# An attention stage set anew in a fused attention and two-layer kernel: q scaled in its cast, row sums inverted in one go, new keys

## The chip, the cores and the metric

The kernel runs on one core of one Trainium2 chip. The metric is the time of one execution on the device in microseconds (us); the kernel before has a median of 741.01 us in three runs (741.01 to 741.36). Five engines work side by side: TensorE (PE, matrix products; PEld is its loading of weights), VectorE (DVE), ScalarE (ACT), GpSimd (POOL) and SyncE (SP), which here issues nearly all DMAs. Each runs its own list of instructions in order and waits on semaphores for the others. SBUF is the working memory with 128 partitions, PSUM the memory that PE writes into, in banks.

## The reference

```
scores = (q @ k.T) / sqrt(64), for 2 x 8 heads of 768 tokens, 64 wide
scores = -1e9 where the six sign bits of q @ proj and of k @ proj differ
attn   = softmax(scores);  x = attn @ v, heads side by side: 1536 x 512
h = x @ w_in (512 x 2048);  x = (h * tanh(softplus(h))) @ w_out
h = x @ w_in2;              out = (h - tanh(h)) @ w_out2
```

## The kernel before, in words

**Products in parts.** Every operand of a product is split into a high part (a cast to a shorter float) and a low part (the operand less its high part), and a product is high x high + high x low + low x high.

**Attention.** Heads are handled in eight pairs g, each with heads h = 0, 1. Transposed q and k of a pair lie as 128 x 768 tiles; `halves_split` (line 413) makes qh, ql, kh, kl from them in halves of 384 columns. For the first pair ScalarE and VectorE do it. For the others GpSimd makes kh, kl and ql, while ScalarE first scales q in place (line 423) and then casts it to qh (line 430). `piece` (line 467) makes three matmuls per half for the sign bits, which go to a tile z. `stack` (line 499) gathers by eight DMAs per head the rows of qh, ql, kh, kl and z into four tiles a, b, c, d, so that a score tile (128 queries x 768 keys) is four matmuls: b,a and d,c for 512 keys, then for 256 (lines 582, 583). They go into the tile s, of which PSUM holds one. A few tiles of the start (`SPLIT_S`) go into two small banks pt instead.

`scores` (line 566): VectorE clamps a tile out of PSUM into a buffer p and takes its row minimum (line 586); ScalarE takes the exponential and the row sums (line 609). `chunk` (line 631): PE transposes three tiles p for one chunk of 128 keys (line 643); then either ScalarE writes the high part ph (line 659) and VectorE the low part pl (line 662), or, in the chunks of `POOL_C`, ScalarE copies to f (line 651) and GpSimd makes ph and pl (line 655). PE multiplies them with the values vt (lines 622, 623), four chunks later. `gather` (line 669) adds the two parts of the result to u; `inverse` (line 681) inverts the row sums of one half of the queries (three small VectorE ops, lines 691 to 695) and spreads them through DRAM by six DMAs (lines 701, 705) into a tile r; `finish` (line 710) multiplies u by r and splits the outcome into xh and xl, on GpSimd save for the last pair.

**Two expert layers.** In blocks of 16 units, with products of seven instead of eight blocks; their weights come as 64-bit integers and are converted (`to_float`, lines 820 to 850), some of it during attention.

**The order.** No engine's list is written by hand. Every step is an `op` with an engine, a cost, a key and what it reads and writes. `Plan.order` (line 196) walks a clock: at each moment it picks, for the engine that can start first, the step with the smallest key among those that can start within `EPS` of the first. Keys of the attention count in ticks (`TICK`, 24 per pair, `at`); `AHEAD` says how many ticks a score tile comes ahead of its transposes, `STACK`, `VALUES`, `LOAD` when in a pair the DMAs and values are due. `LATE`, `LATS`, `LATG` are the latencies that the planner adds between engines; `RATE` and `ISSUE` price DMAs. The numbers at the top of the file thus decide the place of each instruction.

## Time and profile before

| | us |
|---|---|
| median of three runs | 741.01 |
| profiled execution | 740.89 |
| its span, first to last instruction | 739.1 |
| PE busy | 727.7 (98%) |
| PEld busy | 673.6 (91%) |
| VectorE busy | 643.8 (87%) |
| ScalarE busy | 529.7 (72%) |
| GpSimd busy | 179.7 (24%) |

Shares are of the span. Attention fills about the first 230 us, the expert layers the rest; GpSimd works in the first part only. A matmul's row is as long as the matmul is in the engine, and the next one starts before it ends, so its cost is read from start to start. The granted clock of PE is at its higher level in every slice of the page. In a row of the timeline "[0.31 <-POOL kh L375]" says that the engine idled 0.31 us before it, until that instruction of GpSimd.

### The profile page before, as it was taken

To read this page: it belongs to the slowest core of one execution; us is meant where nothing else is said; L and a number is where in the kernel's file an instruction comes from. 1 tells how busy PE (TensorE), PEld (TensorE's weight loads), DVE (VectorE), ACT (ScalarE), POOL (GpSimd) and SP (SyncE) were. 2 spreads that over 40 slices of the span, in tenths; PEclk is the share of its full clock that TensorE was granted. 3 is DMA by queue.
4 is the path that set the end of the run, shared out by engine and by line. 5 is a ranking of instruction groups with operands and counts; after the bars stand their busy time and mean duration, and the time that the engine had idled before them with its cause. 6 is when DMAs were issued, how large, how long until landed. Compare 5 with 4: busy or idle time off the path is not lost.

```text
span 739.1 us, 13094 instructions
## 1 busy us (share of the span) xinstructions
PE 727.7 (98%) x4382; PEld 673.6 (91%) x4382; DVE 643.8 (87%) x1372; ACT 529.7 (72%) x1140; POOL 179.7 (24%) x224
## 2 busy tenths in 40 slices
PE   7999999999999999999999999999999999999998
PEld 4889999999999999999999999998998899999997
DVE  6988998998999999999898899789898775767893
ACT  6989999999997866767676676666565445466660
POOL 5677987988961000000000000000000000000000
PEclk9999999999999999999999999999999999999999
DMA  7775775785562655545655567999986786735621
GB/s 215 184 200 130 204 201 129 204 211 126 156 175 88 231 197 168 172 156 179 204 181 186 185 232 247 330 330 329 350 295 251 270 278 232 244 144 186 222 87 64
DMA packets 59390, 150.96 MB, mean 204 GB/s; under 512 B 7990, under 2 KB 20406, under 8 KB 59324
## 3 DMA queue, kind: packets, MB, share of 16 engines
q1 hardware_dynamic: 58892, 149.65, 63.9%
q8 instruction: 34, 0.56, 0.3%
q10 hardware_dynamic: 432, 0.49, 0.2%
q14 instruction: 32, 0.26, 0.1%
HBM read 88.18 MB, written 43.04 MB: 178 GB/s over the span
## 4 chain that ended last, share of the span: by engine, by line
PE 93%; DVE 2%; DMA 2%; ACT 2%; issue 1%; POOL 0%; ACTq 0%; SPq 0%; DVEq 0%; POOLq 0%
PE pt L1023 11%; PE pt L1025 11%; PE pt L1024 11%; PE pt L643 8%; PE pt L1101 6%; PE pt L1113 6%; PE s L1100 6%; PE pt L1100 6%; PE pt L1338 5%; PE s L582 4%; PE pt L622 4%; PE pt L623 4%; PE s L583 4%; PE s L1338 3%; PE s L1113 3%; DVE p L586 1%
## 5 line engine op out<-in xcount | busy, mean ns | idle before, releaser
L1023 PE MATMUL pt<-xh,a 128*128 128x384 f32 x288 | 96.7, 336 | 0.0
L1025 PE MATMUL pt<-xh,a 128*128 128x384 f32 x288 | 96.7, 336 | 0.0
L1024 PE MATMUL pt<-xl,a 128*128 128x384 f32 x288 | 96.6, 335 | 0.0
L586 DVE TENSOR_SCALAR_CACHE_REDUCE p<-s 128x768 f32<-128x768 f32 x93 | 88.2, 948 | 7.6 <-PE s L583 5.7
L609 ACT ACTIVATE p<-p,mn 128x768 f32<-128x768 f32 x96 | 90.7, 945 | 3.1 <-DVE p L586 2.0
L662 DVE TENSOR_TENSOR pl<-pt,ph 128x384 fp32r<-128x384 f32 x148 | 78.5, 546 | 8.6 <-ACT ph L659 7.6
L643 PE MATMUL pt<-cst,p 128*128 128x128 f32 x576 | 83.8, 272 | 1.1 <-DVE pl L662 1.1
L643 PEld LDWEIGHTS pt<-cst,p 128*128 128x128 f32 x576 | 69.5, 140 | 6.1 <-DVE pl L662 1.4
L659 ACT CAST ph<-pt 128x384 fp32r<-128x384 f32 x148 | 68.8, 484 | 5.2 <-PE pt L622 3.1
L1101 PE MATMUL pt<-gh,o 128*128 128x256 f32 x256 | 71.7, 280 | 0.0
L622 PE MATMUL pt<-ph,vt 128*128 128x384 f32 x192 | 70.4, 367 | 0.3 <-ACT f L651 0.2
L582 PE MATMUL s<-b,a 128*128 128x512 f32 (+1 forms) x186 | 68.2, 367 | 1.1 <-DVE p L586 0.7
L623 PE MATMUL pt<-pl,vt 128*128 128x384 f32 x192 | 64.9, 338 | 0.4 <-DVE pl L662 0.4
L583 PE MATMUL s<-d,c 77*128 77x512 f32 (+3 forms) x186 | 59.3, 340 | 0.6 <-ACT raw L846 0.6
L802 DVE TENSOR_TENSOR gl<-pl,gh 128x384 fp32r<-128x384 f32 x96 | 52.4, 551 | 6.5 <-ACT gh L1047 6.5
L1023 PEld LDWEIGHTS pt<-xh,a 128*128 128x128 f32 x288 | 54.1, 188 | 3.3 <-ACT pl L1042 0.2
L1024 PEld LDWEIGHTS pt<-xl,a 128*128 128x128 f32 x288 | 54.1, 188 | 1.3
L1025 PEld LDWEIGHTS pt<-xh,a 128*128 128x128 f32 x288 | 54.1, 188 | 0.1
L1047 ACT CAST gh<-pl 128x384 fp32r<-128x384 f32 x96 | 48.7, 514 | 2.1 <-DVE pl L802 1.1
L1101 PEld LDWEIGHTS pt<-gh,o 128*128 128x128 f32 x256 | 48.3, 189 | 0.0
L1061 ACT COPY ph<-pt 128x384 f32<-128x384 f32 x56 | 26.9, 481 | 28.7 <-PE pt L1025 28.6
L1100 PE MATMUL pt<-gh,o 128*128 128x512 f32 x128 | 47.2, 391 | 0.0
(301 smaller groups left out, 2080.7 us busy)
## 6 DMA issues: line engine op xcount, KB each, us to landing
w<-w SPq DMA_DIRECT2D x52, 512.0 KB
raw<-in_moe_w_in_dram SPq DMA_DIRECT2D x32, 512.0 KB
raw<-in_moe_w_out_dram SPq DMA_DIRECT2D x32, 512.0 KB
split<-a SPq DMA_DIRECT2D x24, 512.0 KB
a<-split SPq DMA_DIRECT2D x24, 512.0 KB
w<-t SPq DMA_DIRECT2D x32, 256.0 KB
o<-split SPq DMA_DIRECT2D x24, 256.0 KB
b<-kh SPq DMA_DIRECT2D x30, 192.0 KB
```

The source lines that it names most:

```text
L582: nc.tensor.matmul(o, a()[:, tok], b_()[:, kc], start=True, stop=False)
L583: nc.tensor.matmul(o, c_()[used, tok], d_()[used, kc], start=False, stop=True)
L586: nc.vector.tensor_scalar(out=out, in0=in_, scalar1=MASKED, scalar2=None, op0=ALU.min, op1=ALU.min, accum_out=low)
L609: lambda: nc.scalar.activation(out=p(), in_=p(), func=AF.Exp, bias=mn(), scale=-1.0, accum_out=sm()[:, h, t:t + 1],),
L622: nc.tensor.matmul(o()[:, :HB], vt()[:, c, :], ph()[:, :HB], start=(c == 0), stop=False)
L623: nc.tensor.matmul(o()[:, :HB], vt()[:, c, :], pl()[:, :HB], start=False, stop=(c == NT - 1))
L643: nc.tensor.transpose(pt()[:, t * P:(t + 1) * P], ps[t]()[:, c * P:(c + 1) * P], ident)
L1023: nc.tensor.matmul(o, tl()[:, 0, c], at_(0, kk), start=start and kk == 0, stop=False, skip_group_check=not start)
L1024: nc.tensor.matmul(o, tl()[:, 0, c], at_(1, kk), start=False, stop=False, skip_group_check=not start)
L1025: nc.tensor.matmul(o, tl()[:, 1, c], at_(0, kk), start=False, stop=kk == 1, skip_group_check=not start)
L1100: nc.tensor.matmul(a()[:, n, :], w()[:, y, c], flat[x][:, :SEG], start=st, stop=sp)
L1101: nc.tensor.matmul(r()[:, 0, rest], w()[:, y, c], flat[x][:, SEG:], start=st and d % 2 == 0, stop=sp, skip_group_check=True)
```

## The change

The high part of q is written by ScalarE with the scale in the same instruction, for every pair and not only the first, and its low part is made by VectorE from the unscaled q. The row sums of both halves of a pair are inverted together (12 columns instead of 6, four stores and two spreads for a pair), but for the last pair; both halves of a pair are then finished after its second half. One more chunk per head goes by way of GpSimd, save in the last pair. The identity for the transposes is copied to a tile of its own, and the two columns of constants that stay in use are loaded once more. There are eight p buffers instead of six, and one wide r instead of two. The numbers of the planner for the attention are set anew. `MOVED` is empty, so the code that it guards emits nothing.

```
-POOL_C = ((1, 4), (4,))
+POOL_C = ((1, 4), (1, 4))
-SPLIT_S = (1, 3, 5)
+SPLIT_S = (1, 2, 4)
-T_BUFS, P_BUFS, U_BUFS = 4, 6, 3
+T_BUFS, P_BUFS, U_BUFS = 4, 8, 3
+MOVED = ((), ())
-Q_SCALE = "ACT"
-EPS = 0.0
+EPS = 0.145
-AHEAD = 9
+AHEAD = 11
...
-STACK = 12
-VALUES = 11
-LOAD = 15
...
+STACK = 17
+VALUES = 16
+LOAD = 14
...
-            if nm == "q" and g:
-                if Q_SCALE == "ACT":
-                    op("ACT", 0.42, k0 - 0.1, lambda c=c: nc.scalar.activation(out=raw()[:, c], in_=raw()[:, c], func=AF.Copy, scale=-SCALE), [], [(raw, i)])
...
-                op("ACT", 0.42, k0, lambda c=c: nc.scalar.copy(th()[:, c], raw()[:, c]), [(raw, i)], [(th, i)])
-            elif nm == "q":
+            if nm == "q":
                 op(
                     "ACT", 0.38, k0, release=Q_REL if (g, i) == (0, 1) else 0.0, fn=
                     lambda c=c: nc.scalar.activation(out=th()[:, c], in_=raw()[:, c], func=AF.Copy, scale=-SCALE),
...
-            if nm == "q" and not g:
+            if nm == "q":
                 op(
-                    "DVE", 0.47 if g == 0 else 0.6, k0 + 0.1,
+                    "DVE", 0.47, k0 + 0.1,
                     lambda c=c: nc.vector.scalar_tensor_tensor(
                         out=tl()[:, c], in0=raw()[:, c], scalar=-SCALE, in1=th()[:, c],
                         op0=ALU.mult, op1=ALU.subtract,
...
-        ("u", "u", U_BUFS), ("r", "r", 2), ("rt", "rt", 2), ("small", "mn mn2 sums", 6),
+        ("u", "u", U_BUFS), ("r", "r", 1), ("rt", "rt", 2), ("small", "mn mn2 sums", 6),
...
+            op("POOL", 0.25, 6.0, lambda: pool_copy(ident, land[:, 0, 0:P]))
...
-    def inverse(g, half, key):
+    def inverse(g, halves, key):
...
+        i0, nh = halves[0], len(halves)
+        rd, n = rds[i0], nh * 2 * TB
...
+            lambda: nc.vector.tensor_tensor(out=used(), in0=sm()[:, :, i0:i0 + nh], in1=tiny[:, :, :nh], op=ALU.add),
...
-                nc.sync.dma_start(out=r()[h * D:(h + 1) * D], in_=d[h:h + 1].to_broadcast([D, HB]))
+                nc.sync.dma_start(out=r()[h * D:(h + 1) * D, i0 * HB:(i0 + nh) * HB], in_=d[h:h + 1].to_broadcast([D, nh * HB]))
...
-                if h == 1:
-                    inverse(g, half, at(NT * n - 2))
+                if h == 1 and (half or g == len(pairs) - 1):
+                    inverse(g, (half,) if g == len(pairs) - 1 else (0, 1), at(NT * n - 2))
...
-                    if h == 1:
+                    if h == 1 and g == len(pairs) - 1:
                         finish(g, half, u, key + 0.3)
+                    elif h == 1 and half:
+                        for i in range(2):
+                            finish(g, i, us[i], key + 0.3 + i)
...
-    nc.scalar.dma_start(out=cst, in_=cst_d)
+    nc.scalar.dma_start(out=land[:, 0, 0:P + 66], in_=cst_d)
+    nc.scalar.dma_start(out=cst[:, 0:2], in_=cst_d[:, P:P + 2])
```

On PE, in the start: from the score tiles of the first queries to the first transposes (pt<-cst,p before; pt<-ident,p in the changed file, whose lines are numbered a little lower here). Before:

```order
L478 MATMUL pt<-qh,pjh 64x384
L479 MATMUL pt<-qh,pjl 64x384
L480 MATMUL pt<-ql,pjh 64x384
L478 MATMUL pt<-kh,pjh 64x384
L479 MATMUL pt<-kh,pjl 64x384
L480 MATMUL pt<-kl,pjh 64x384
L643 MATMUL pt<-cst,p 128x128 x6
```

And after:

```order
L471 MATMUL pt<-qh,pjh 64x384
L472 MATMUL pt<-qh,pjl 64x384
L473 MATMUL pt<-ql,pjh 64x384
L471 MATMUL pt<-kh,pjh 64x384
L472 MATMUL pt<-kh,pjl 64x384
L473 MATMUL pt<-kl,pjh 64x384
L471 MATMUL pt<-kh,pjh 64x384
L472 MATMUL pt<-kh,pjl 64x384
L473 MATMUL pt<-kl,pjh 64x384
L644 MATMUL pt<-ident,p 128x128 x3
```

A second piece of k, of the next pair, now stands ahead of the first transposes, and only three of these follow before the next score tile.

On PE, in the fourth pair, between two score tiles (s<-b,a for 512 keys is the first matmul of a tile). Before:

```order
L582 MATMUL s<-b,a 128x512
L583 MATMUL s<-d,c 128x512
L582 MATMUL s<-b,a 128x256
L583 MATMUL s<-d,c 128x256
L622 MATMUL pt<-ph,vt 128x384
L623 MATMUL pt<-pl,vt 128x384
L622 MATMUL pt<-ph,vt 128x384
L623 MATMUL pt<-pl,vt 128x384
L643 MATMUL pt<-cst,p 128x128 x3
L582 MATMUL s<-b,a 128x512
```

And after, between two tiles of the fifth pair:

```order
L575 MATMUL s<-b,a 128x512
L576 MATMUL s<-d,c 128x512
L575 MATMUL s<-b,a 128x256
L576 MATMUL s<-d,c 128x256
L619 MATMUL pt<-ph,vt 128x384
L620 MATMUL pt<-pl,vt 128x384
L644 MATMUL pt<-ident,p 128x128 x3
L619 MATMUL pt<-ph,vt 128x384
L620 MATMUL pt<-pl,vt 128x384
L644 MATMUL pt<-ident,p 128x128 x3
L575 MATMUL s<-b,a 128x512
```

Two products of the values and two runs of transposes lie between the tiles here, where two products and one run lay; each pair of the new order, from the third to the seventh, has the same distances between its tiles.

On GpSimd before, in the fourth pair, where the low part of q is made:

```order
L454 TENSOR_TENSOR kl<-k,kh 128x384 x2
L719 TENSOR_TENSOR u<-u,r 128x384
L454 TENSOR_TENSOR ql<-q,qh 128x384
L375 TENSOR_SCALAR xh_134<-u 128x384
L375 TENSOR_SCALAR ph<-f 128x384
L726 TENSOR_TENSOR xl_138<-u,xh_134 128x384
```

And on VectorE after, where it is made now:

```order
L579 TENSOR_SCALAR p,mn<-s 128x768
L437 SCALAR_TENSOR_TENSOR ql<-q,qh 128x384
L663 TENSOR_TENSOR pl<-pt,ph 128x384
L579 TENSOR_SCALAR p,mn<-s 128x768
L676 TENSOR_TENSOR u<-pt,f 64x384
L663 TENSOR_TENSOR pl<-pt,ph 128x384
```

The subtraction stands between two clamps of score tiles now.

## Rows read from the trace of the kernel before

**Rows 1.** Windows: us, PE, PEld, DVE, ACT, POOL busy (count), PEclk, DMA share, GB/s.

```profile
0.00:25.00 25.00, 18.78 (x85) 13.47 (x85) 18.64 (x47) 18.03 (x35) 15.52 (x25) 1.00 0.82 222
25.00:60.00 35.00, 34.42 (x221) 30.40 (x221) 29.92 (x68) 32.65 (x74) 27.19 (x35) 1.00 0.74 185
60.00:225.00 165.00, 164.85 (x1088) 151.74 (x1087) 153.24 (x342) 159.32 (x354) 135.11 (x164) 1.00 0.64 166
225.00:245.00 20.00, 19.55 (x125) 18.52 (x124) 19.57 (x45) 15.06 (x34) 1.85 (x2) 1.00 0.44 151
245.00:739.00 494.00, 490.09 (x2872) 459.44 (x2870) 422.45 (x875) 304.62 (x648) 0.00 (x0) 1.00 0.64 220
```

**Rows 2.** Timeline of PE, 113 to 117 us: start, duration, instruction [idle before].

```profile
113.90 0.49 PE L643 MATMUL pt<-cst,p 128*128 128x128 f32 x3
114.14 0.48 PE L582 MATMUL s<-b,a 128*128 128x512 f32 x1
...
114.93 0.34 PE L622 MATMUL pt<-ph,vt 128*128 128x384 f32 x1
115.11 0.34 PE L623 MATMUL pt<-pl,vt 128*128 128x384 f32 x1
...
115.64 0.49 PE L643 MATMUL pt<-cst,p 128*128 128x128 f32 x3
116.15 0.50 PE L582 MATMUL s<-b,a 128*128 128x512 f32 x1
```

**Rows 3.** Timeline of DVE, the clamp of the tile at 114.14.

```profile
115.13 0.96 DVE L586 TENSOR_SCALAR_CACHE_REDUCE p<-s 128x768 f32<-128x768 f32 x1 [0.49 <-PE s L583]
```

**Rows 4.** Groups by form, 45 to 210 us: count, busy us, mean ns, idle before.

```profile
L423 ACT ACTIVATE q<-q 128x384 f32<-128x384 f32 x10 | 5.5, 550 | 0.0
...
L662 DVE TENSOR_TENSOR pl<-pt,ph 128x384 fp32r<-128x384 f32 x108 | 57.4, 546 | 6.7 <-ACT ph L659 6.0
...
L691 DVE TENSOR_TENSOR rd<-sums,tiny 128x6 f32<-128x6 f32 x12 | 2.7, 228 | 0.0
L695 DVE STREAM_TRANSPOSE rt<-rd 128x32 f32<-128x32 f32 x12 | 2.5, 204 | 0.0
L694 DVE RECIPROCAL rd<-rd 128x6 f32<-128x6 f32 x12 | 2.2, 181 | 0.1
...
L655 POOL TENSOR_TENSOR pl<-f,ph 128x384 fp32r<-128x384 f32 x36 | 37.5, 1041 | 1.8
L375 POOL TENSOR_SCALAR ph<-f 128x384 fp32r<-128x384 f32 x36 | 18.9, 524 | 17.2 <-ACT f L651 14.2 <-PE pt L623 2.0 <-PE pt L643 0.5
...
L454 POOL TENSOR_TENSOR ql<-q,qh 128x384 fp32r<-128x384 f32 x12 | 12.0, 1017 | 0.0
```

**Rows 5.** Line 444 alone: count, ns minimum/median/maximum, first and last start.

```profile
L444 DVE SCALAR_TENSOR_TENSOR ql<-q,qh x2: 553/556/559, 5.3 to 13.0; 128x384 fp32r<-128x384 f32 x2
```

**Rows 6.** Window of one pair, first score tile to first score tile.

```profile
120.65:147.97 27.32, 27.32 (x183) 25.09 (x182) 25.11 (x57) 26.51 (x61) 22.96 (x29) 1.00 0.75 191
```

**Rows 7.** Timeline of PE in the start.

```profile
16.30 0.39 PE L480 MATMUL pt<-kl,pjh 128*64 128x384 f32 x1 [1.47 <-POOL kl L454]
...
21.24 0.55 PE L643 MATMUL pt<-cst,p 128*128 128x128 f32 x3 [1.14 <-DVE pl L662]
```

**Rows 8.** Timeline of POOL in the start: both halves of kl.

```profile
15.25 2.07 POOL L454 TENSOR_TENSOR kl<-k,kh 128x384 fp32r<-128x384 f32 x2 [0.56 <-DMA d<-kl]
```

**Rows 9.** Timeline of SP: start and length of an issue.

```profile
9.26 0.62 SPq L381 DMA_DIRECT2D d<-kl  x1
...
111.94 0.84 SPq L381 DMA_DIRECT2D c<-z  x1
```

**Rows 10.** Timeline of PE: the first score tile of the fifth pair.

```profile
120.65 0.48 PE L582 MATMUL s<-b,a 128*128 128x512 f32 x1
```

**Rows 11.** Lines 600 and 838 alone, columns as in rows 5.

```profile
L600 DVE TENSOR_TENSOR mn<-mn,mn x3: 145/151/1037, 13.4 to 22.5; 128x1 f32<-128x1 f32 x3
...
L838 DVE SCALAR_TENSOR_TENSOR w<-raw,w x6: 668/680/1074, 54.8 to 193.4; 128x512 uint32<-128x512 uint32 x6
```

More of the change, by code (lines that the diff above doesn't have):

```diff
@@ L63 @@
 SPARE = 1
-LATE = 0.22
-LATS = 0.15
-LATG = 0.5
+LATE = 0.28
+LATS = 0.2
+LATG = 0.6
 LATF = 0.3
-TICK = 1.11
-T_ATT = 8.0
-M0 = 7.0
-AHEAD = 9
+TICK = 1.1
+T_ATT = 7.0
+M0 = 2.0
+AHEAD = 11
 PV_LAG = 4
 PIECE = 2.5
-STACK = 12
-VALUES = 11
-LOAD = 15
-FIRST = (0.0, 1.0, 2.0, 6.0)
-V_REL = 15.0
-Q_REL = 9.5
-Z_REL = 12.5
+STACK = 17
+VALUES = 16
+LOAD = 14
+FIRST = (1.0, 0.0, 2.0, 6.0)
+V_REL = 12.0
+Q_REL = 8.0
+Z_REL = 9.5
 FILL = 3
@@ L369, in tile_lsh_attention_moe @@
     hot = plan.pools["f"].tile([P, XB], F32R, tag="f", name="hot")
+    land = plan.pools["w32"].tile([P, 2, DM], F32, tag="w3", name="land")
+    pj = land[:, 0, P + 2:P + 66]
     def x_tok(which, kk, t0, n):
@@ L572, in scores @@
         p, mn = buf("p", "p", [P, S]), buf("small", "mn", [P, 1])
-        sm = sums[g, half]
+        sm = sums[g]
         rows = (False, True) if g or h else (False, True, "bits")
@@ L610, in scores @@
                 out=p(), in_=p(), func=AF.Exp, bias=mn(), scale=-1.0,
-                accum_out=sm()[:, h, t:t + 1],
+                accum_out=sm()[:, h, half, t:t + 1],
             ),
-            [mn, (p, 0), (p, 1)], [p, (sm, h, t)],
+            [mn, (p, 0), (p, 1)], [p, (sm, h, half, t)],
         )
+        if t in MOVED[half]:
+            pr = buf("p", "p", [P, S], F32R)
+            dma(P * S * 4, key + MOVE_KEY, lambda: pr().bitcast(F32), p, [p], [pr], rate=FAST)
+            return pr
         return p
@@ L679, in gather @@
         )
-    def inverse(g, half, key):
-        sm, rd, rt = sums[g, half], rds[half], buf("rt", "rt", [P, 32])
-        tok = ("rd", half)
-        r = rs[g, half] = buf("r", "r", [P, HB])
-        n = 2 * TB
-        d = scratch.tile([2, HB], F32, name=f"inv{g}_{half}")
-        used = lambda: rd[:, :n].rearrange("p (h t) -> p h t", h=2)
+    def inverse(g, halves, key):
+        rt = buf("rt", "rt", [P, 32])
+        i0, nh = halves[0], len(halves)
+        rd, n = rds[i0], nh * 2 * TB
+        tok = ("rd", i0)
+        if (g, "r") not in rs:
+            rs[g, "r"] = buf("r", "r", [P, S])
+        r, sm = rs[g, "r"], sums[g]
+        d = scratch.tile([2, nh * HB], F32, name=f"inv{g}_{i0}")
+        used = lambda: rd[:, :n].rearrange("p (h i t) -> p h i t", h=2, i=nh)
         op(
             "DVE", 0.15, key,
-            lambda: nc.vector.tensor_tensor(out=used(), in0=sm(), in1=tiny, op=ALU.add),
-            [(sm, h, t) for h in range(2) for t in range(TB)], [tok],
+            lambda: nc.vector.tensor_tensor(out=used(), in0=sm()[:, :, i0:i0 + nh], in1=tiny[:, :, :nh], op=ALU.add),
+            [(sm, h, i, t) for h in range(2) for i in halves for t in range(TB)], [tok],
         )
@@ L718, in finish @@
         op(
-            eng, cost, key + 0.2, lambda: e.tensor_tensor(out=u(), in0=u(), in1=r(), op=ALU.mult),
-            [r], [(u, 0), (u, 1)],
+            eng, cost, key + 0.2, lambda: e.tensor_tensor(out=u(), in0=u(), in1=r()[:, half * HB:(half + 1) * HB], op=ALU.mult),
+            [(r, half)], [(u, 0), (u, 1)],
         )
@@ L749, in tile_lsh_attention_moe @@
         us = []
+        sums[g] = buf("small", "sums", [P, 2, 2, TB])
         for half in range(2):
-            sums[g, half] = buf("small", "sums", [P, 2, TB])
             us.append(buf("u", "u", [P, HB]))
```

39 lines of the change are left out of this document (19 added, 20 removed).

## The prediction, made before the changed kernel ran

> **What bounds the kernel now.** I read the table of windows first, because the page's share of busy time mixes stages. The reader is to see the column of PE [rows 1]: after the first 25 us PE idles 0.58 us in 25 to 60, 0.15 in 60 to 225, 0.45 in 225 to 245, and 3.9 in all that follows. The attention stage, which is all that the change rewrites, is therefore bound by TensorE with ScalarE close behind (159.32 of 165 us busy, 97%), VectorE at 93% and GpSimd at 82%. PE runs the same matmuls before and after, in number and shape (the two orders count the same), so the change can only give back what PE loses now: 6.2 us of idle time in the first 25 us, some 1.2 us of idle time until 245, and stalls that hide inside "busy".
>
> The hidden stalls were the second reading, in the timeline of PE. A score tile (four matmuls into the one bank s) must wait until VectorE has clamped the tile before it out of that bank. [Rows 2] show two neighbours: the three transposes before the tile at 114.14 take 0.24 us from start to start, those before the tile at 116.15 take 0.51; the difference, 0.27 us, is a wait, although the row shows almost no idle time. Tile to tile that is 116.15 - 114.14 = 2.01 us with a clamp that waited for nothing but its matmuls (it began at 115.13 after 0.49 us of idle VectorE, [rows 3]). So 2.01 us is the shortest distance at which two tiles of s can follow each other. Between 60 and 225 there are ten such stretched runs of transposes, of 0.1 to 0.3 us, 2.3 us together. The worst stand where the order puts two tiles only 1.7 us of PE work apart: a tile takes 0.79 us there (114.14 to 114.93), a product 0.18, a run of three transposes 0.24.
>
> **The change part by part.** The profiled execution took 740.89 us, 1.8 us more than its span of 739.1; the median of the runs shown is 741.01, 0.12 above it. The sum is made against 740.89.
>
> *q.* Fourteen half tiles lose a ScalarE pass of 550 ns [rows 4] and get the scale in the cast that remains. GpSimd loses fourteen subtractions of 1017 ns, VectorE gets fourteen of 556 ns [rows 5]. *Pooled chunks.* Fourteen more chunks of the transposed scores go through GpSimd: VectorE loses fourteen times 546 ns, GpSimd gains 524 + 1041 ns each [rows 4]. *Row sums.* In seven of eight pairs one inversion replaces two: VectorE loses 7 x (228 + 181 + 204) = 4.3 us, and SP loses 42 issues. Per pair of heads, against the period measured between two first tiles (27.32 us, [rows 6]): ScalarE 26.51 - 2 x 0.55 = 25.4 us (97 to 93%); VectorE 25.11 + 2 x (0.556 - 0.546) - 0.61 = 24.5 (92 to 90%); GpSimd 22.96 + 2 x 1.565 - 2 x 1.017 = 24.1 (84 to 88%). None of this is on PE's path by itself: it is hidden behind PE, which fills the period. It gives the clamps more room. If that cover went, GpSimd is still 3.2 us short of the period.
>
> *Keys, steady part.* In the new order, behind the start, no two tiles of s are closer than 2.03 us of PE work, by the pitches of [rows 2] and the order (the piece shown: 0.79 + 2 x 2 x 0.18 + 2 x 0.24 + 0.09 that the first run adds to the product behind it); one pair of tiles in the last pair of heads stands at 1.7. So the 2.01 us need no longer stretches PE, unless VectorE is late. I take back 1.6 of the 2.3 us and leave 0.7, since many distances are now only 0.02 to 0.06 above the need and a subtraction of 546 ns in front of a clamp overdraws that. Bounds: 2.3 us saved, or 5 lost (below).
>
> *Keys, 25 to 60.* 0.58 us of idle PE [rows 1]: the same two engines are late there. I take 0.5 back; bounds 0.6 saved, 0.6 lost (the same stalls at other places).
>
> *Keys, end of attention.* In 225 to 245 PE idles 0.45 us. The old order mixes first matmuls of the expert layer into the last attention chunks, the new one leaves them behind nearly all of these, so they no longer cover waits there, but they stand ready behind. Taken 0.4 back; bounds 0.45 saved, 0.9 lost (twice the present idle time).
>
> *Start.* The new order moves a second three-matmul piece of the next k ahead of the first transposes. That piece waits for the second half of kl, which GpSimd ends at 15.25 + 2.07 = 17.32 [rows 8]; now PE waits only for the first half, until 16.30 [rows 7]. GpSimd's two ops start when the DMA issued at 9.26 [rows 9] has landed, and the change does not move that. PE thus starts its transposes about 1.0 us later, but with 3 x 0.17 us more done: 0.45 us lost. VectorE's next clamp begins later by nearly as much. In return the third tile goes to a bank of its own (that wait goes, but PE then only waits earlier for kl), and the stall of 1.14 us at 21.24 [rows 7] has three score tiles put ahead of it. Two new distances of 1.7 us cost 0.3 each. Sum: 0.45 + 0.6 - 1.14 = about 0. Bounds: 1.1 saved, 1.0 lost. The extra small load of two columns on ScalarE's queue delays q by one issue, beside the longer chain over k to the first tile; the copy of the identity runs while GpSimd waits for q. Both are taken at nothing, with 0.6 us (a DMA issue of [rows 9] is 0.62) as the upper end.
>
> *DMA.* The operands of the next pair are now written later: PE has 7.6 us of work between the last piece of q and the first score tile that needs it, 9.7 us before (counts of the order times the pitches). Now the last z issue is at 111.94 and the tile at 120.65 [rows 9, 10], 8.7 us; 2.1 less leaves 6.6, and the slowest landing that the trace bounds is under 6.0 (issued at 9.26, its waiter runs at 15.25, in the crowded start; [rows 8, 9]). Cost nothing, and if it were 1 us short, 7 pairs would cost 7 us. Eight p buffers instead of six let scores run two ticks further ahead; no row shows a wait for p, so nothing.
>
> Sum: 0 - 0.5 - 1.6 - 0.4 = -2.5, so 738.4 profiled and **738.5 us** as a median.
>
> **Rivals.**
> *The port (slower).* The new subtraction on VectorE reads two operands from SBUF, the one it replaces reads one from PSUM. [Rows 11] show what can happen to such an op: a minimum of two columns takes 145 to 151 ns, and 1037 when it began beside GpSimd's work. Price: up to 0.89 us for each of fourteen; the clamp behind it is late by that, less the 0.02 to 0.2 us of room between tiles. If half of them hit and cost PE 0.7 us each, that is 4.9 us: 743.4. It decides from about 4 hits on (4 x 0.7 gives back the 2.5). For it: GpSimd is at 88% and reads SBUF all the time. Against: the old two-operand ops of the six conversions run at a median of 680 ns with a maximum of 1074, so most are not hit. The Trainium skill, SBUF — State Buffer (Who interferes with whom), says that a DVE instruction with two SBUF inputs contends with a GpSimd instruction that reads SBUF, and that whoever starts first holds the pair for the whole instruction; by that rule the reciprocal's addition and this subtraction are exposed and the clamp is not, and the trace agrees (1037 against 151 ns).
> *No change.* What is gained at the clamps is lost in the start: PE waits in order for kl, VectorE idles meanwhile, and nothing later gives it back, 1.0 lost, with half of the steady stalls kept: 738.5 + 1.0 + 1.0 = 740.5. For it: PE runs in order. Against: VectorE's list up to 28 us holds no more work than before.
> *More.* The start gains too: the stalls at 16.30 (1.47 us) and 21.24 overlap with other work: 736.
>
> **How the numbers follow.** Forecast 0.48, port 0.19, no change 0.25, more 0.08. The forecast's own range is 736.8 to 740.0. No change, as far as a measurement of this kernel can tell, is within 0.2%, 1.5 us of 741.01: 739.5 to 742.5. Of the forecast 0.44 lies below 739.5; with the eight of "more" and a little of "no change" faster is 0.53. Same takes most of "no change" and the rest of the forecast, 0.27; slower the port and a small rest, 0.20. The range, 735.8 to 743.2, leaves out the worse half of the port and the depth of "more".
>
> **What would show it.** Right: in the windows PE idles under 0.3 us in 25 to 60, runs of three transposes before a score tile keep 0.24 us, the first transposes begin near 17.5, and ScalarE is near 93% from 60 to 225. Wrong: subtractions of q on VectorE with a mean over 700 ns; score tiles whose releaser is a DMA; GpSimd above 95%, with products that wait for its pl; a new stall of PE above 1 us between 17 and 30 or where the expert layer begins.

## The result: 749.69 us, 1.1% slower

The changed kernel took 749.69 us (median of four runs, 748.93 to 750.13), the kernel before 741.18 beside it (741.01 to 742.56): a ratio of 1.011, 95% interval 1.0092 to 1.0127. The forecast was 738.5, the range ended at 743.2. The profiled execution took 748.93 us with a span of 747.1.

The table of windows of the changed kernel, in the columns and stretches of [rows 1]:

```profile
0.00:25.00 25.00, 17.89 (x70) 12.18 (x70) 16.78 (x43) 14.96 (x29) 13.74 (x24) 1.00 0.73 195
25.00:60.00 35.00, 34.06 (x218) 30.05 (x219) 33.08 (x67) 31.82 (x72) 25.72 (x33) 1.00 0.81 199
60.00:225.00 165.00, 163.21 (x1063) 146.45 (x1061) 151.23 (x312) 153.18 (x337) 145.50 (x179) 1.00 0.70 170
225.00:245.00 20.00, 19.29 (x123) 17.00 (x122) 19.86 (x47) 16.38 (x37) 4.10 (x6) 1.00 0.15 52
245.00:747.00 502.00, 498.00 (x2917) 467.48 (x2915) 428.60 (x886) 310.51 (x656) 0.00 (x0) 1.00 0.64 219
```

The loads of the helpers came out close to the forecast: from 60 to 225 us ScalarE is busy 93% (forecast 93%, before 97%), VectorE 92% (90%, 93%), GpSimd 88% (88%, 82%). PE starts fewer matmuls in every stretch of attention all the same: 70 against 85 in the first 25 us, 1063 against 1088 from 60 to 225. From 25 to 60 us it idles 0.94 us, 0.58 before.

Since idle time is nearly invisible in these rows, I measured the loss by pitch: for each matmul the time to the start of the next one, less what is usual for its shape (231, 175, 118 and 109 ns for 512, 384, 256 and 128 columns), summed. "Start" is the work up to the first 14 us of pitch, "pairs" from there to 186, "turn" to 222 (last pair and entry into the expert layer), "rest" what follows. The four right columns are of one profiled execution each, medians of all executions; the ratios leave out three executions that lay over 1.5% above the fastest of their kernel, one of e4 and two of e13, whose profiled one (770.16 us) is among them. The expectations of the runs count these losses in another way, which gives some 2.4 us less for the pairs (3.6 for before instead of 6.0).

Kernels with the same instructions in the start still differ there from one execution to another: before lost 9.6 us, e15 11.4. PE's granted clock differs with it. In e15's execution it is at its lower level, 1.2 GHz (0.50 in the windows), from 14.9 to 21.7 us; in before's it is at its higher one, 2.4 GHz, through all of the start, although PE waits there for the same kh and kl. The profiled executions of e1 to e4, e7, e8, e10, e12, e13, e15 and e17 have such a stretch in the start; those of before, the changed kernel, e5, e6, e9, e11, e14, e16 and e18 have none. So a start is judged by the times and by what landed when, not by one entry.

| kernel | median us | ratio to before (95%) | start | pairs | turn | rest |
|---|---|---|---|---|---|---|
| before | 741.18 | | 9.6 | 6.0 | 1.6 | 2.2 |
| changed | 749.69 | 1.011 (1.0092 to 1.0127) | 12.0 | 10.0 | 3.1 | 3.0 |
| e1 constants behind q | 747.61 | 1.0073 (1.0048 to 1.0097) | 11.3 | 9.5 | 2.8 | 3.0 |
| e2 e1, low q without a second source | 746.37 | 1.0052 (1.0029 to 1.0075) | 12.5 | 8.4 | 2.7 | 3.0 |
| e3 e1, fewer pooled chunks | 746.20 | 1.0056 (1.0039 to 1.0073) | 13.2 | 8.9 | 3.2 | 2.1 |
| e4 e1, q as before | 748.03 | 1.0093 (1.0066 to 1.0119) | 11.4 | 10.9 | 2.8 | 1.8 |
| e5 constants copied | 746.11 | 1.0070 (1.0056 to 1.0085) | 9.2 | 8.7 | 2.7 | 3.1 |
| e6 e5, old keys | 748.08 | 1.0097 (1.0082 to 1.0113) | 9.7 | 12.0 | 3.9 | 2.8 |
| e7 before, new keys | 761.32 | 1.0275 (1.0238 to 1.0312) | 12.8 | 20.3 | 2.6 | 2.4 |
| e8 before, extra load | 745.16 | 1.0063 (1.0040 to 1.0086) | 13.8 | 5.9 | 1.6 | 2.3 |
| e9 e5, inverse per half | 745.20 | 1.0051 (1.0037 to 1.0065) | 9.6 | 10.3 | 2.2 | 2.2 |
| e10 joint inverse, old keys | 745.12 | 1.0046 (1.0029 to 1.0062) | 10.5 | 8.0 | 3.9 | 2.8 |
| e11 q path, old keys | 749.58 | 1.0110 (1.0094 to 1.0126) | 10.0 | 13.8 | 3.2 | 2.9 |
| e12 q path, old order | 749.13 | 1.0088 (1.0066 to 1.0109) | 11.6 | 13.3 | 2.4 | 2.6 |
| e13 before, one key nudged | 761.10 | 1.0208 (1.0161 to 1.0254) | 12.4 | 28.1 | 6.3 | 2.4 |
| e14 e5, one key nudged | 751.34 | 1.0128 (1.0114 to 1.0142) | 10.3 | 12.5 | 2.6 | 4.8 |
| e15 joint inverse, old order | 748.08 | 1.0083 (1.0066 to 1.0099) | 11.4 | 11.2 | 2.0 | 2.4 |
| e16 e5, other forms on VectorE | 751.92 | 1.0130 (1.0093 to 1.0166) | 9.5 | 10.3 | 4.0 | 8.2 |
| e17 e13, other form of the mask | 769.04 | 1.0353 (1.0311 to 1.0394) | 10.8 | 25.0 | 6.5 | 8.2 |
| e18 before, scale left out | 741.84 | 0.9988 (0.9968 to 1.0008) | 10.0 | 6.1 | 2.4 | 2.3 |

By this count the changed kernel lost 2.4 us in the start, 4.0 in the pairs, 1.5 at the turn and 0.8 behind.

### The profile page after: what moved, and what is told of

Its sections match the earlier page's. It is cut to its first block, busy times and chain, and to the rows that moved or that the text cites. A ratio compares the mean times of both kernels' runs of the same rounds, so it can differ in the third digit from the quotient of the medians.

```text
span 747.1 us, 13013 instructions
## 1 busy us (share of the span) xinstructions
PE 732.4 (98%) x4382; PEld 673.2 (90%) x4382; DVE 649.5 (87%) x1351; ACT 526.9 (71%) x1126; POOL 189.1 (25%) x239
## 4 chain that ended last, share of the span: by engine, by line
PE 81%; DVE 5%; DMA 4%; POOL 3%; issue 3%; SPq 1%; ACT 1%; ACTq 0%; DVEq 0%; POOLq 0%
PE pt L1031 11%; PE pt L1033 11%; PE pt L1032 10%; PE pt L1109 6%; PE pt L1121 6%; PE s L1108 6%; PE pt L1108 6%; PE pt L1346 5%; PE pt L644 4%; PE s L1346 3%; PE s L1121 3%; PE s L575 3%; PE s L576 2%; PE pt L620 2%; PE pt L619 2%
## 5 line engine op out<-in xcount | busy, mean ns | idle before, releaser
L644 PE MATMUL pt<-ident,p 128*128 128x128 f32 x576 | 88.8, 273 | 0.1
L663 DVE TENSOR_TENSOR pl<-pt,ph 128x384 fp32r<-128x384 f32 x134 | 71.8, 546 | 6.0 <-ACT ph L660 5.2
L644 PEld LDWEIGHTS pt<-ident,p 128*128 128x128 f32 x576 | 70.8, 140 | 6.9 <-ACT f L652 2.3
L619 PE MATMUL pt<-ph,vt 128*128 128x384 f32 x192 | 72.6, 378 | 1.1 <-ACT f L652 0.9
L575 PE MATMUL s<-b,a 128*128 128x512 f32 (+1 forms) x186 | 70.1, 377 | 3.3 <-DVE p L579 2.8
L660 ACT CAST ph<-pt 128x384 fp32r<-128x384 f32 x134 | 63.9, 483 | 4.0 <-PE pt L619 3.2
L656 POOL TENSOR_TENSOR pl<-f,ph 128x384 fp32r<-128x384 f32 x58 | 59.1, 1019 | 2.7
L575 PEld LDWEIGHTS s<-b,a 128*128 128x128 f32 x186 | 35.5, 191 | 13.0 <-DVE p L579 8.4
```

Of the source, the lines that this page charges most:

```text
L575: nc.tensor.matmul(o, a()[:, tok], b_()[:, kc], start=True, stop=False)
L619: nc.tensor.matmul(o()[:, :HB], vt()[:, c, :], ph()[:, :HB], start=(c == 0), stop=False)
L644: nc.tensor.transpose(o, x, ident.bitcast(F32))
```

## The start: a load of 1 KB in front of q

ScalarE's timeline (start, duration, engine or its DMA queue ACTq, line, operation; in brackets the idle time before and what ended it). Before, then in the changed kernel:

```profile
1.20 0.90 ACTq L408 DMA_DIRECT2D q<-in_q_dram  x2
4.79 0.52 ACT L434 ACTIVATE qh<-q 128x384 fp32r<-128x384 f32 x1 [2.33 <-DMA q<-in_q_dram]
```

```profile
1.17 0.46 ACTq L1415 DMA_DIRECT2D cst<-cst_dram  x1
...
1.69 0.90 ACTq L411 DMA_DIRECT2D q<-in_q_dram  x2
7.57 0.52 ACT L427 ACTIVATE qh<-q 128x384 fp32r<-128x384 f32 x1 [4.63 <-DMA q<-in_q_dram]
```

And PE's first score tile:

```profile
12.39 0.63 PE L575 MATMUL s<-b,a 128*128 128x512 f32 x1
```

The extra load takes 0.46 us to issue, and q's loads begin 0.49 us later than before (1.20). q itself comes 2.8 us later: its cast runs at 7.57, before at 4.79. SP issues v (384 KB) at 1.64 and a weight tile (512 KB) at 2.11 or 2.12 in both kernels; before, q's loads began ahead of v, and now they begin behind it. The first score tile starts at 12.39 instead of 9.30. What the two DMA queues moved between 3 and 4 us (q1 is SP's, q10 ScalarE's; packets, MB, share of 16 engines), before and after:

```profile
q1 hardware_dynamic: 154, 0.21, 56.6%
q10 hardware_dynamic: 155, 0.19, 51.6%
```

```profile
q1 hardware_dynamic: 184, 0.29, 76.8%
q10 hardware_dynamic: 188, 0.03, 16.9%
```

So SP's loads took the place of q's.

**e1.** The small load is issued after q's two loads; nothing else moves.

```
-    nc.scalar.dma_start(out=cst[:, 0:2], in_=cst_d[:, P:P + 2])     # ahead of the planned program
+    n_q += o in q_first
+    if n_q == 2: nc.scalar.dma_start(out=cst[:, 0:2], in_=cst_d[:, P:P + 2])
```

> The changed kernel with one thing moved: the second small load of the constants (two columns) is issued on ScalarE's queue behind the two loads of q, no longer in front of them. Every engine's order is otherwise that of the changed kernel. Theory 1 (the start): the q halves are issued 0.49 us later in the changed kernel (1.69 against 1.20) and so fall behind the loads of v and of the first raw weights in the DMA engines; q is waited for until 7.57 instead of 4.79. Then this run gives back 2 to 2.8 us of the 8.5: 747 to 747.7, and ScalarE casts q near 4.8. Rival: the start is absorbed later, since VectorE has to do the same work anyhow; then it gives back under 0.7 us.

ScalarE in e1:

```profile
1.20 0.91 ACTq L412 DMA_DIRECT2D q<-in_q_dram  x2
2.15 0.45 ACTq L1431 DMA_DIRECT2D cst<-cst_dram  x1
4.89 0.52 ACT L428 ACTIVATE qh<-q 128x384 fp32r<-128x384 f32 x1 [2.44 <-DMA q<-in_q_dram]
...
10.11 0.57 ACT L455 ACTIVATE c<-pt,cst 13x384 fp32r<-13x384 f32 x1 [2.37 <-DMA cst<-cst_dram]
```

q is back at 4.89, and now the 1 KB is what is late: issued at 2.15, it lands at about 10, and the bit rows of c and d wait for it. PE then idles 2.69 us in the first score tile, and its granted clock is at 1.2 GHz from 12.4 to 15.8. The time, 747.61 us, is still in the range of theory 1.

**e5.** No second load: VectorE copies the two columns out of the landing tile.

```
-    nc.scalar.dma_start(out=cst[:, 0:2], in_=cst_d[:, P:P + 2])
+    nc.vector.tensor_copy(cst[:, 0:2], land[:, 0, P:P + 2])
```

> The changed kernel without its second load of constants: VectorE copies the two columns (the bias and the scale of the bit rows) out of the landing tile, one small instruction before the cast of pj; the planned order is untouched. In the run with that load put behind q's, the q casts came back to 4.89 us, but the two columns then landed at 10.1 us and the bit rows of c and d waited for them (ACT 2.37 us idle). Theory A (the split constant load makes the whole loss of the start): no wait on either, first score products run through from 9 to 9.5 us, start's excess over the pitch 9.6 us as before against 12.0, so the time falls by 2.0 to 2.5 us against the changed kernel, to 747.2 (ratio 1.0075). Rival B (the new start keys, SPLIT_S and FIRST, make the loss): kl's second half still late, excess stays over 11, time 749 (ratio over 1.0095).

q's loads are issued at 1.19 and its cast runs at 4.48:

```profile
1.19 0.90 ACTq L411 DMA_DIRECT2D q<-in_q_dram  x2
4.48 0.52 ACT L427 ACTIVATE qh<-q 128x384 fp32r<-128x384 f32 x1 [2.03 <-DMA q<-in_q_dram]
```

The start's loss is 9.2 us (9.6 in before). The ratio falls from 1.011 to 1.0070, and the two intervals do not overlap; theory A had 1.0075. By the ratios e5 is hardly better than e1 (1.0073), so what e1's wait for the 1 KB costs can't be seen in the times.

**e8**, from the other side: the kernel before with such a load into a tile that nobody reads.

```
     nc.scalar.dma_start(out=cst, in_=cst_d)
+    nc.scalar.dma_start(out=spare[:, 0:2], in_=cst_d[:, P:P + 2])
```

> The kernel before with one more load of two columns of the constants (1 KB, into a spare tile that nobody reads) issued on ACT's queue between the constants and q's first halves; order untouched. Start theory: q's issue 0.45 to 0.5 us later, its landing 2 to 3 us later because v and raw of SP's queue get in front, first score tile 12 instead of 9.3 us, time 743.5 to 744.5 (ratio 1.003 to 1.004). Rival (the first stage's slack hides a late q as the prediction had it: at most 0.6 us): 741.2 to 742.3.

```profile
1.17 0.46 ACTq L1407 DMA_DIRECT2D even<-cst_dram  x1
...
1.68 0.90 ACTq L408 DMA_DIRECT2D q<-in_q_dram  x2
7.92 0.52 ACT L434 ACTIVATE qh<-q 128x384 fp32r<-128x384 f32 x1 [4.99 <-DMA q<-in_q_dram]
```

The same delay, and 4.3 us on the median (745.16 against 740.87), more than the 743.5 to 744.5 expected. A part of it may be the clock's: its mean was 0.993 to 0.998 in all eight executions, and in the profiled one it is at 1.2 GHz from 20.2 to 23.6. Taken away the load gave back 0.4%, some 3 us; added it cost 4.3. It is thus shown from both sides that the load makes the start's loss, or most of it; a part of the new keys (SPLIT_S, FIRST) is not seen, and could hide in the scatter of the starts.

## The pairs: a gain that was not there, and two edits that cost

**e18: ScalarE's relief alone.** The scale is left out, so the scores of these pairs are other ones.

```
-    ... nc.scalar.activation(out=raw()[:, c], in_=raw()[:, c], func=AF.Copy, scale=-SCALE) ...
+    ... lambda: None ...                     # the order of everything else is the old one
```

> The kernel before in its own order with ACT's scaling of q left out for pairs 2 to 8 (the scores of these pairs are unscaled and of the other sign) and nothing put in its place: what the 0.94 us per pair taken off ACT are worth by themselves, without VectorE's added subtractions. The prediction's steady term (ACT's relief brings back a part of 2.3 us of stalls): 739.0 to 740.5. Rival (ACT's time is cover, the clamp on VectorE ends the waits): 741 to 742.

```profile
60.00:225.00 165.00, 164.38 (x1077) 149.89 (x1076) 154.63 (x337) 155.46 (x342) 134.42 (x163) 1.00 0.64 166
```

ScalarE falls from 159.32 to 155.46 us in this stretch, and the time does not move (0.9988, 0.9968 to 1.0008). ScalarE's time was cover; the waits at the score tiles do not end on it.

**e12: the low part on VectorE, old order.** As e18, and VectorE's instruction stands where GpSimd's stood. It differs from e18 only in the engine that subtracts (and in the scale, which the cast now has). The place was set for GpSimd; another one on VectorE was not tried.

```
-    lambda c=c, e=e: e.tensor_tensor(out=tl()[:, c], in0=raw()[:, c], in1=th()[:, c], op=ALU.subtract)
+    lambda c=c: nc.vector.scalar_tensor_tensor(out=tl()[:, c], in0=raw()[:, c], scalar=-SCALE, in1=th()[:, c], ...)   # q
```

> The kernel before in its own planned order, instruction for instruction, with the q path of pairs 2 to 8 exchanged in place: ACT's scale left out and its cast made the scaled cast, the low part done by VectorE's scalar_tensor_tensor at the place in the program where GpSimd's subtraction stood; constants and start as before, inverse per half. Theory C (the q path replanned cost 8 us because any order that is planned anew, with keys that were set for another one, is 3 to 8 us worse in the pairs): 739 to 742.5. Theory D (the q path itself: VectorE's subtractions at 0.75 to 0.95 us beside GpSimd delay the clamps): 745 or more.

VectorE between two clamps in the second pair, in the kernel before (L586) and in e12 (L589):

```profile
51.51 0.96 DVE L586 TENSOR_SCALAR_CACHE_REDUCE p<-s 128x768 f32<-128x768 f32 x1
...
53.56 0.41 DVE L830 TENSOR_SCALAR w<-raw 128x512 uint32<-128x512 uint32 x1
53.89 0.94 DVE L586 TENSOR_SCALAR_CACHE_REDUCE p<-s 128x768 f32<-128x768 f32 x1
```


```profile
53.67 0.96 DVE L589 TENSOR_SCALAR_CACHE_REDUCE p<-s 128x768 f32<-128x768 f32 x1
...
54.67 0.77 DVE L454 SCALAR_TENSOR_TENSOR ql<-q,qh 128x384 fp32r<-128x384 f32 x1
55.36 0.54 DVE L665 TENSOR_TENSOR pl<-pt,ph 128x384 fp32r<-128x384 f32 x1
55.83 0.66 DVE L466 TENSOR_SCALAR z<-pt,cst 26x384 fp32r<-26x384 f32 x1
56.42 0.79 DVE L454 SCALAR_TENSOR_TENSOR ql<-q,qh 128x384 fp32r<-128x384 f32 x1
57.13 1.22 DVE L833 TENSOR_SCALAR w<-raw 128x512 uint32<-128x512 uint32 x1
58.27 0.94 DVE L589 TENSOR_SCALAR_CACHE_REDUCE p<-s 128x768 f32<-128x768 f32 x1
```

And what PE does behind it:

```profile
59.28 0.50 PE L585 MATMUL s<-b,a 128*128 128x512 f32 x1 [1.70 <-DVE p L589]
```

From clamp to clamp 4.60 us; before, the same two begin 2.38 us apart. The 2.2 us more are the two subtractions (1.4 from start to start) and the bit mask (L833, before L830), 0.81 longer. VectorE had idle time elsewhere in the pair, but a clamp is due every 2 us or so, and there the slack is some tenths. Shorter waits of the same kind stand at 90.28 (1.15 us), 145.97 (0.78) and 202.48 (0.83). Summed by pitch, some 6 of the 7.3 us that e12's pairs lose more than before's are lost in front of score tiles. Its 749.13 us are theory D's (745 or more).

**e15: the joint inverse, old order.** Half 0's three VectorE instructions, stores and spreads go; its three finishing instructions stand right ahead of half 1's.

```
+        if two and half == 0: ...          # nothing issued
+            nc.vector.tensor_tensor(out=used()[:, :, i], in0=x(), in1=tiny, op=ALU.add)   # for both halves
+        fin(...)                            # half 0: kept until half 1's first finishing instruction
```

> The kernel before in its own planned order with the joint inverse put in by hand for pairs 1 to 7: the first half's three VectorE instructions, stores and spreads left out, the second half's made for both (one small VectorE addition more than in the changed kernel), and the first half's three finishing instructions on GpSimd put right ahead of the second half's. Theory C: 740 to 742.5, since GpSimd has slack in that order and only the first half's finish is late. Theory A (joint inverse costs by itself through six GpSimd instructions in a row, 5 us): 744 to 746, with f's copies waiting behind them.

GpSimd in e15 (L754, L376 xh and L761 finish a half; L656 makes a pooled chunk's low part), then PE:

```profile
54.59 1.17 POOL L754 TENSOR_TENSOR u<-u,r 128x384 f32<-128x384 f32 x1
55.85 0.90 POOL L376 TENSOR_SCALAR xh<-u 128x384 fp32r<-128x384 f32 x1
56.83 1.02 POOL L761 TENSOR_TENSOR xl<-u,xh 128x384 fp32r<-128x384 f32 x1
57.80 1.01 POOL L754 TENSOR_TENSOR u<-u,r 128x384 f32<-128x384 f32 x1
58.77 1.01 POOL L656 TENSOR_TENSOR pl<-f,ph 128x384 fp32r<-128x384 f32 x1
```

```profile
59.83 0.45 PE L624 MATMUL pt<-pl,vt 128*128 128x384 f32 x1 [0.61 <-POOL pl L656]
```

Half 0's finish and the first instruction of half 1's stand ahead of a pl that PE needs. Such a stall of 0.6 us returns at 94.52, 122.68 and 179.73; summed by pitch, 3.7 of the 5.2 us that e15's pairs lose more than before's are lost at a pl of GpSimd. Its 748.08 us are beyond the 744 to 746 of theory A. Both edits cost at the full clock as well: the executions with a mean granted clock of 1.000 took 745.51 and 748.71 us in e12, 746.18 to 747.74 in e15.

The changed kernel shows a like pattern, one step longer. From 82.15, where half 0's multiply begins, GpSimd there works for 13 us with hardly a gap; the last part of it:

```profile
87.97 1.69 POOL L723 TENSOR_TENSOR u<-u,r 128x384 f32<-128x384 f32 x1
...
90.11 0.51 POOL L378 TENSOR_SCALAR xh<-u 128x384 fp32r<-128x384 f32 x1
90.59 1.01 POOL L656 TENSOR_TENSOR pl<-f,ph 128x384 fp32r<-128x384 f32 x1
91.56 1.02 POOL L730 TENSOR_TENSOR xl<-u,xh 128x384 fp32r<-128x384 f32 x1
92.53 1.33 POOL L858 TENSOR_TENSOR w<-w,raw 128x512 uint32<-128x512 uint32 x1
93.82 0.52 POOL L378 TENSOR_SCALAR ph<-f 128x384 fp32r<-128x384 f32 x1
94.42 1.01 POOL L656 TENSOR_TENSOR pl<-f,ph 128x384 fp32r<-128x384 f32 x1
```

ScalarE, whose copy f needs a buffer that this pl frees:

```profile
95.47 0.48 ACT L652 COPY f<-pt 128x384 f32<-128x384 f32 x1 [1.47 <-POOL pl L656]
```

PE, first at the product whose PSUM bank f empties, then at the next score tile, whose clamp is late behind it:

```profile
96.00 0.44 PE L619 MATMUL pt<-ph,vt 128*128 128x384 f32 x1 [0.47 <-ACT f L652]
...
97.84 0.50 PE L575 MATMUL s<-b,a 128*128 128x512 f32 x1 [0.21 <-DVE p L579]
```

By pitch, the stalls above 0.25 us in the pairs of this trace make 3.4 us, 1.1 in the kernel before. This chain, which returns at 180.30 and 182.15, is 2.0 of them. Another 1.1 stand in front of two score tiles (50.29 and 53.40), whose clamps follow a subtraction of q that takes 1.2 us. The remaining growth of the pairs is in smaller stalls.

**e10, e11, e6: the edits under the old keys, planned anew.** e6 is e5 with every planner constant of the kernel before; e10 is e6 with the old q path, e11 is e6 with the inverse per half.

```
-POOL_C = ((1, 4), (1, 4))   -SPLIT_S = (1, 2, 4)   -EPS = 0.145   -AHEAD = 11   ...
+POOL_C = ((1, 4), (4,))     +SPLIT_S = (1, 3, 5)   +EPS = 0.0     +AHEAD = 9    ...      # e6
```

> The kernel of e5_const_copied with all planner constants of the kernel before (the table POOL_C with one pooled product fewer, SPLIT_S, rates, latencies, ticks, start offsets, first-load order, conversion keys, six p buffers), planned anew: what is left of the change is q scaled at its high part with VectorE's low part, the joint inverse of both halves, the fp32r identity, and the constants copied. Theory A (the new keys make the loss of 3.6 us in the pairs and 1.5 at the turn): within 1.5 us of before, 740 to 743, GpSimd no longer behind in front of f's copies. Rival B (the code makes it: the port of the q low parts, or the joint inverse with both finishes in a row on GpSimd): still 745 to 747, with late products behind the two finishes.

> Old keys, old q path (ACT scale and cast, GpSimd low part), joint inverse and both finishes together, constants copied, planned anew: the joint inverse alone against the kernel before. Theory A (joint inverse is the cost): 744 to 747 (ratio 1.004 to 1.008), GpSimd's run of six finishing instructions ahead of products that the matmuls wait for. Rival B (the q path is the cost): 740 to 742.

> Old keys, q scaled at its high part with VectorE's low part, inverse per half as before, constants copied, planned anew: the q path alone against the kernel before. Theory A (joint inverse is the cost): 738 to 741.5, as the prediction had it for this edit. Rival B (the q path is the cost: 0.75 us for each subtraction on VectorE beside GpSimd's stream instead of 0.56, clamps late): 744 to 748. If both this and the joint inverse alone cost 3 us or more, neither edit is to blame by itself, and it is any new order against keys set for another one.

The joint inverse alone costs 0.46%, the q path alone 1.10%, both 0.97%. So each edit costs in both orders tried, and they do not add up. e6 and e11 lie above the ranges of both their theories, e10 in that of its theory A. By the last clause of e11's expectation neither edit is to blame by itself, only the new order; but e12 and e15 show a cost of each in the old order too.

**e7: the new keys with the old code**, and **e13, e14: one key nudged.**

```
-LATE = 0.22      +LATE = 0.25      # e13, kernel before
-LATE = 0.28      +LATE = 0.25      # e14, kernel of e5
```

> The kernel before with the planner constants of the changed kernel (all but the buffer counts) and none of its code: old q path (ACT scale and cast, GpSimd low part), inverse per half, one constant load. Theory A (keys): the pairs cost 3 to 5 us more, time 745 to 747 (ratio 1.004 to 1.008). Rival B (code): within 1 us of before, 741 to 742.5. With both of q's GpSimd subtractions and the wider pooled table GpSimd has most to do here, so a loss above 747 would say that the keys only pay with q's low part taken off GpSimd.

> The kernel before with one planner constant nudged: the latency charged between engines 0.25 for 0.22 us; no code of the kernel changed, planned anew. Theory C (any replanned order is worse than the one that the keys were set for): 744 to 750, the pairs' excess 6 us or more against 3.6. Rival (the order is robust, and it is the edits that cost): within 1.5 us of before, 740 to 743.

> The kernel of e5_const_copied with the same constant at 0.25 for 0.28 us, planned anew. Theory C: its own keys are no better than any others, so it lands 744 to 750, on either side of 746.1, and the spread between the two is the size of the planner's chance. Rival (the new keys are set for the new code as the old ones for the old): clearly worse than e5, 749 or more.

The new keys are not worse in themselves: with the new code they are some 2 us better than the old (e5 against e6), with the old code 20 us worse (745 to 747 had been expected). It is not the old q path alone that makes this: e4 below has it under the new keys, with the joint inverse, and took 748.03 us. e14's 751.34 us are its rival's (749 or more). A latency changed by 0.03 us, with no other edit, costs 2% in the kernel before, where I had expected 744 to 750.

Not all of this is the order itself. The six executions of e13 follow their mean granted clock, from 750.18 us at 1.000 to 770.16 at 0.984; in the last one PE waits 3.1 to 3.6 us at three score tiles, each time behind a bit mask that VectorE was held in (next section), and around each of these waits the clock falls to 1.2 GHz (from 121.7, 152.4 and 217.3 us on). Those of e7 go from 756.11 us at 1.000 to 765.91 at 0.989. At the full clock the nudge thus cost 8.5 us in the one execution that had it, about what the q path costs; an order is worth as much here as an edit, and more where the clock falls with it.

## Is VectorE held by GpSimd?

The subtractions on VectorE grew beside GpSimd. In the changed kernel (min/median/max in ns; [rows 5] have 553/556/559):

```profile
L437 DVE SCALAR_TENSOR_TENSOR ql<-q,qh x16: 541/856/1252, 8.1 to 195.0; 128x384 fp32r<-128x384 f32 x16
```

**e2**: e1 with the low parts of pairs 2 to 8 as a scaled copy with an accumulator; the subtraction of the high part is left out.

```
-    nc.vector.scalar_tensor_tensor(out=tl()[:, c], in0=raw()[:, c], scalar=-SCALE, in1=th()[:, c], op0=ALU.mult, op1=ALU.subtract)
+    nc.vector.tensor_scalar(out=tl()[:, c], in0=raw()[:, c], scalar1=-SCALE, scalar2=None, op0=ALU.mult, op1=ALU.min, accum_out=cst[:, 2:3])
```

> As the run before (constants behind q), and the low part of q for the pairs 2 to 8 is made by a VectorE instruction with one SBUF input and an accumulator (the scaled q itself; the subtraction of the high part is left out, so the values are not the reference's). The order is that of the changed kernel. Theory 2 (the port): the subtraction with two SBUF inputs waits for GpSimd (median 856 ns against 556 uncontended) and makes the clamps late; without it the steady part from 60 to 225 us gives back 1.5 to 2.5 us beyond the run before. Rival (GpSimd too full, or the order too tight): under 0.7 us.

```profile
L438 DVE TENSOR_SCALAR_CACHE_REDUCE ql<-q x14: 529/548/553, 27.2 to 193.9; 128x384 fp32r<-128x384 f32 x14
```

This form did not grow beside GpSimd, and the median falls by 1.2 us against e1, with ratios whose intervals overlap: less than theory 2 had (1.5 to 2.5 us), more than its rival (under 0.7). So the stretching of q's subtractions is real; by the medians it is the smaller part of the loss.

**e16, e17**: the bit mask of the weight words, tensor_scalar with one source in SBUF, grew as well, in e13 to 4561 ns where its median is 418. Both kernels give it as scalar_tensor_tensor with a column of threes; e16 is e5 with e2's form besides.

```
-    nc.vector.tensor_scalar(out=t(), in0=word(1), scalar1=0x07FFFFFF, scalar2=3, ...)
+    nc.vector.scalar_tensor_tensor(out=t(), in0=word(1), scalar=0x07FFFFFF, in1=three[:, 0:1].to_broadcast([P, DM]), ...)
```

> The kernel of e5_const_copied, same order, with the two kinds of VectorE instruction that read and write SBUF alone and grew beside GpSimd put into other forms: q's low parts of pairs 2 to 8 as a scaled copy with an accumulator (the subtraction of the high part is left out, so these low parts are wrong), and the bit mask of the weight words as scalar_tensor_tensor with a column of threes in place of tensor_scalar (0.67 us by the row of its neighbour instead of 0.41, same values). Theory P (VectorE held by GpSimd makes most of the pairs' loss): VectorE's excess over its quiet durations falls from 7.8 us to under 3, the pairs' excess from 6.3 to 4 us or so, time 743 to 744.5. Rival O (the order and the six finishing instructions in a row make it, not the held instructions): 745.5 to 747.

> The kernel of e13_before_nudged, same order, with the bit mask of the weight words as scalar_tensor_tensor (same values). In e13 three of the seven masks lasted 4.1 to 4.6 us instead of 0.41, each to within 0.3 us of the end of a run of GpSimd instructions without a gap. Theory P (the form with one SBUF source waits for such a run to end, the form with two takes turns with it): no mask over 1.6 us, the three stalls of 3.3 to 3.6 us before score tiles gone, time 748 to 752 against 761. Rival (whatever reads SBUF there waits for the run): masks still over 3 us, time 758 or more.

In e17 the rival came true: it is not the form. VectorE and GpSimd there:

```profile
141.60 4.49 DVE L830 SCALAR_TENSOR_TENSOR w<-raw,even 128x512 uint32<-128x512 uint32 x1
146.12 0.69 DVE L838 SCALAR_TENSOR_TENSOR w<-raw,w 128x512 uint32<-128x512 uint32 x1
```

```profile
140.21 1.00 POOL L454 TENSOR_TENSOR ql<-q,qh 128x384 fp32r<-128x384 f32 x1
141.17 1.01 POOL L719 TENSOR_TENSOR u<-u,r 128x384 f32<-128x384 f32 x1
...
144.08 0.99 POOL L726 TENSOR_TENSOR xl<-u,xh 128x384 fp32r<-128x384 f32 x1
145.04 0.51 POOL L375 TENSOR_SCALAR vt<-v 128x384 fp32r<-128x384 f32 x1
```

The new form waits as long as the old one: the mask ends at 146.09, 0.54 us after the last of a run of GpSimd instructions without a gap has ended (145.55). e16 (751.92 us, above both of its ranges) is inconclusive on the pairs: the masks last longer with nothing beside them (684 against 418 ns median), and its rest lost 5 us in the expert layers, where no GpSimd works.

**e3, e4, e9: other shares between the engines** under the new keys: one pooled chunk per pair fewer; the old q path; the inverse per half.

```
-POOL_C = ((1, 4), (1, 4))      +POOL_C = ((1, 4), (4,))                                    # e3
-    if nm == "q":              +    if nm == "q" and g: (scale and cast on ACT, low part on POOL)   # e4
-    if h == 1 and (half or g == len(pairs) - 1):   +    if h == 1: inverse(g, (half,), ...)          # e9
```

> As the first run (constants behind q), with the pooled chunks of the kernel before: one chunk less per head goes by way of GpSimd. The planner sets the order anew. Theory 3 (GpSimd too full): the two waits for ScalarE's copy f (0.47 and 0.45 us idle, each with a late clamp behind it, some 2.2 us together) go, and the time falls by 1.5 to 3 us against the first run. Rival (port, or keys): under 1 us, or slower, since VectorE gets 0.55 us back per head.

> As the first run (constants behind q), with q of the pairs 2 to 8 as in the kernel before: scaled in place and cast by ScalarE, low part by GpSimd; the planner sets the order anew. GpSimd then has 24.1 + 2.0 = 26.1 us of work in a pair of 27.3. If the port is the cause: 1 to 2 us faster than the first run. If GpSimd's load is: slower than the first run by 1 us or more.

> The kernel of e5_const_copied (new keys, q low part on VectorE, constants copied) with the inverse and the finish done per half again as before: each half's row sums inverted at the end of its own turn, its GpSimd multiply, cast and subtraction behind it, so that GpSimd has three instructions (2.6 us) in a row instead of six; planned anew. Theory A (joint inverse: six finishing instructions in a row on GpSimd delay its products, f's copies and then the clamps): the pairs' excess falls from 6.3 to about 4 us, time 743 to 744.5. Rival B (port and order of VectorE: the q subtractions between the clamps): the pairs stay at 6 us or more, time 745.5 to 748, with VectorE's three small instructions and two stores per pair added back.

None of them gets the pairs back to 6 us, and none reaches what its theory asked for: e3 is 1.4 us below e1, e4 0.4 above it, e9 0.9 below e5. e9's pairs lost 10.3, more than e5's 8.7; its better time comes from the turn and the rest. No version was found that beats the kernel before.

## Why the prediction was wrong

- **Start**, "Both are taken at nothing, with 0.6 us (a DMA issue of [rows 9] is 0.62) as the upper end": failed. The price was taken as one issue; the issue is 0.49 us and the landing 2.8 us later, because q lost its place ahead of v and the weights (0.03 MB moved between 3 and 4 us instead of 0.19). Worth 3 to 4 us (e5, e8). The other sums of the start (kl, banks) drown beside it.
- **Keys, steady part**, "I take back 1.6 of the 2.3 us": failed, and it is the step that gave the forecast its sign. It rested on more room at the clamps from less load on ScalarE and VectorE. The loads came nearly as worked out, and so did the distances: from 60 to 225 us no two tiles of s follow each other in less than 2.04 us. But ScalarE's relief is worth nothing (e18), and an average of 92% on VectorE says nothing of the interval between two clamps, where the subtraction stands (e12). The pairs cost 4.0 us instead of giving 1.6 back. The bound of the text, "5 lost", held. The 2.01 us are not the shortest distance either: before has two tiles of s 1.93 us apart (64.10 to 66.03).
- **Keys, 25 to 60**, 0.5 taken back: failed. PE idles 0.36 us more there, within the bound of 0.6.
- **Joint inverse**, counted as 4.3 us less for VectorE and 42 issues less for SP, and nothing else: failed. What it moves are six GpSimd instructions, now close together, ahead of products (e15).
- **End of attention**, -0.4: failed, 1.5 lost at the turn by pitch, which takes in the last pair. No experiment changes the turn alone, so its cause stays open.
- **DMA of the next pair's operands**, nothing: held; no large stall of a score tile in the pairs has a transfer as releaser.
- **The port**, the rival given 0.19: its sign came true, subtractions with a mean of 905 ns (45 to 210 us) where "a mean over 700 ns" was the mark. Its price did not: it put a loss of 4.9 us there, and e2 gives 1.2 by the medians. The Trainium skill, SBUF — State Buffer (Who interferes with whom), exempts the tensor_scalar form that writes its accumulator; the trace agrees (529 to 553 ns in e2). That whoever starts first holds the pair of ports for the whole instruction is less than what e17 shows, where the hold outlasts several instructions.

What stays open: the trace of the changed kernel gives 2.0 us to the chain behind GpSimd and 1.1 to clamps behind q's subtractions, but the rest of the 5 us behind the start is in smaller stalls and at the turn, and how much of it is the order as such is not shown. Each edit alone costs 3 to 8 us depending on the order, and orders with none of the edits differ by 20 at the median, with the clock in it, so no sum of parts is to be had from these runs. Nor is it shown why the clock fell in some executions and not in others of the same kernel.

## What to carry on

Price a load put ahead of another by what gets in front of the delayed one in the other queue, not by its issue. Where one instruction recurs with a fixed period and its engine feeds PE, look at the interval between two of them, not at the engine's busy share. And where a planner sets the order, an edit that only moves load can lose more by the new order than it saves: put it into the old order first, unchanged, to see its own price. Where the executions of one kernel scatter, read their granted clocks before putting the scatter down to anything else.
